# A ConvNeXt V2 block on one core: PSUM tiles of 2, 1 and 1 banks for the expansion, and a new order of the tensor engine's work inside a block

## The chip, the core and the metric

The kernel runs on one core of a Trainium2 chip. A core has five engines that each work through a queue of their own in program order: TensorE (PE, matrix products, with its weight loads shown apart as PEld), VectorE (DVE), ScalarE (ACT), GpSimd (POOL) and SyncE (SP), which here only issues DMAs. Matrix products land in PSUM, a small memory of 8 banks, each of which holds 512 float32 numbers in every partition; ACT and DVE read it. The metric is the device time of one execution in microseconds (us), as the median of several runs; lower is better.

## The reference

The input is one image of 512 by 512 pixels with 96 channels. Cut to what matters:

```python
xp = pad(x)                                        # one pixel all round
out = sum(xp[:, i:i+H, j:j+W, :] * dw[i, j] for i in range(3) for j in range(3))
h = layernorm(out, axis=-1)                        # over the 96 channels, eps 1e-5
h = gelu(einsum('bhwc,ce->bhwe', h, w1))           # 96 -> 384 channels
gx = sqrt((h * h).sum(axis=(1, 2)) + 1e-6)         # one number per channel, over ALL pixels
nx = gx / (gx.mean(axis=-1) + 1e-6)
h = grn_gamma * (h * nx) + grn_beta + h
return x + einsum('bhwe,ec->bhwc', h, w2)          # 384 -> 96 channels
```

The sum of squares over all pixels splits the work into two passes: nothing of the second product can start before every pixel has been through the gelu.

## The kernel before

The image is cut into 128 blocks of four rows (`GR = 4`, `NBLK = 128`), 2048 pixels each.

**Pass one** walks over slots `s` (the loop at line 721). A slot does the convolution of one block and, some slots later in the life of a block, each further stage of it: the slot in which a stage runs is put down beforehand in a table (`put`, lines 687 to 714), and `get(kind)` asks for the blocks that are due. So one slot holds the convolution of block `s`, the statistics of an earlier block, the normalising of a still earlier one, and the expansion (`mlp`) of one earlier again. Every engine's instructions are kept in program order (`InOrder`), so the order of the lines in the slot body (lines 779 to 816) is the order on the engine.

- Convolution: `conv_taps` gives three bursts of 24 small matmuls (64 by 32 tiles of the array) into three PSUM banks of the pool `psY`, and `evac`, one ACT copy of those banks to `y_bf`. After bursts 0 and 1 it issues `pe.drain()`.
- LayerNorm: POOL squares `y_bf` (`stage_sq`), PE sums over channels (`stage_stats`, 24 small matmuls), a short chain on POOL and DVE makes 1/sigma, SP carries it through memory to all partitions, and POOL multiplies (`stage_norm`). The normalised block is written to memory and read back transposed (`stage_write`, `stage_read`).
- Expansion: 96 to 384 channels in three groups of 128 (`NCH = 3`), over four quarters of 512 pixels. Two quarters, or three, are made channel-major (`cm_quads`: three in two blocks of three, two in the others), the rest pixel-major. `pair(j)` makes the first two quarters of channel group `j`: two matmuls into a two-bank tile `U` of the pool `psU`, which has two such tiles, and one gelu of 1024 columns into `gsh`. `rest(n)`, three times, makes the rest in the same manner into `gm`. A block thus fills 12 banks in six two-bank tiles, each with one ACT instruction.
- Squares: DVE takes the statistics of channel-major quarters (`squares`, `squares_rest`); the pixel-major ones are squared by PE (`gram_mms`: 12 matmuls for a block with three channel-major quarters, 24 for one with two), one slot later.

PSUM in pass one is full: one bank for sums and Gram (`SG`), four for `psU`, three for `psY`.

The body of a slot with an expansion, before, is

```python
conv(0); pair(0); pair(1)
squares(0)
conv(1); spread_out(); turn_x(s + 2)
pair(2); squares(1)
conv(2); evac()
rest(0); squares(2); stats
rest(1); gram of the block before
rest(2); squares_rest()
```

**Pass two** (line 898) takes the blocks again. Only the first quarter's gelu was stored; the other three are made anew (`recompute_units`, three units `fresh(j)` of a block, each three matmuls and one gelu of 1536 columns), then `stage_mm2` multiplies with the scaled `w2` in four sub-steps of 12 by 4 matmuls, and DVE adds the residual `xb` that POOL prepared. `pace` (line 330), called after each sub-step, says how many units are to have been issued by then: `LEAD` is 8 units at the start, `even` rises with the sub-steps, and `advance` issues what is missing. The last two blocks (`is_res`) are kept on chip and come first in pass two; their units are made at the end of pass one, with a tile of `psU`.

Of the kernel before, what the change touches and what calls it, by code (L numbers as in the profile page):

```python
# [9 lines left out]
ACTF = mybir.ActivationFunctionType  # L10
# [43 lines left out]
def kernel(  # L54
# [33 lines left out]
    def is_res(q):  # L88
        return q >= NBLK - RES
# [13 lines left out]
    def quad(flat_ap, t):  # L103
        return flat_ap.rearrange("p r (t g m) -> p t g r m", t=NQ, m=MB)[:, t]

    def quad_out(flat_ap):
        return flat_ap.rearrange("p (g r m) -> p g r m", r=GR, m=MB)
# [52 lines left out]
    with ExitStack() as p1:  # L160
# [2 lines left out]
        gmpool = p1.enter_context(tc.tile_pool(name="gm", bufs=3))  # L163
        bstpool = p1.enter_context(tc.tile_pool(name="bst", bufs=2))
        psS = p1.enter_context(tc.tile_pool(name="psS", bufs=1, space=bass.MemoryType.PSUM))
        psU = p1.enter_context(tc.tile_pool(name="psU", bufs=2, space=bass.MemoryType.PSUM))
        pc = p1.enter_context(ExitStack())
        psY = pc.enter_context(tc.tile_pool(name="psY", side="right", bufs=1, space=bass.MemoryType.PSUM))
        xinpool = pc.enter_context(tc.tile_pool(name="xin", side="right", bufs=4))
# [84 lines left out]
        def recompute_units(q):  # L254
            nk = kept_quads(q)
            ynt = grp[q]["ynt"]

            def fresh(j):
                if j == 0:
                    grp[q]["made"] = late.gr.tile([128, NCH, (NQ - 1) * QW], bf16, name="gr")  # L260
                if is_res(q):
                    U = psU.tile([128, 2, QW], f32, name="U")
                else:
                    U = late.psU2.tile([128, NQ - 1, QW], f32, name="U2")
                for t in range(nk, NQ):
                    pe.matmul(quad_out(U[:, t - nk, :]), lhsT=w1p[:, j * 128:(j + 1) * 128],
                               rhs=quad(ynt[:], t), start=True, stop=True)
                n = (NQ - nk) * QW
                act.activation(out=grp[q]["made"][:, j, :n], in_=U[:].rearrange("p k w -> p (k w)")[:, :n],
                                func=ACTF.Gelu_apprx_tanh)  # L270

            return [lambda j=j: fresh(j) for j in range(NCH)]

# [55 lines left out]

        def pace(n, sub):  # L330
            due = sum(1 for v in todo if v <= n + 1) if sub == NSUB - 1 else 0
            even = LEAD + (n * NSUB + sub + 1) * (total + 2 - LEAD) / (NSUB * NBLK)
            advance(max(due, even), n + PRE)

        SG = psS.tile([128, 2 * NS + NCH * 128], f32, name="SG")
# [6 lines left out]
                pe.matmul(J[:, k % NI, :], lhsT=zrow[:, :128], rhs=zrow[:], start=True, stop=True)  # L342

        busy(FILL[0])
        Ud = psU.tile([128, 2, W], f32, name="U")[:, 0, :NI * 9].rearrange("p (i k) -> p i k", i=NI)
        for i in range(NI):
            dve.tensor_copy(out=dwx[:, i], in_=dw9[:, None, chans(i)].to_broadcast([9, GR, 32]))
            pe.matmul(Ud[:, i, :], lhsT=dwx[:, i].rearrange("p q c -> p (q c)"), rhs=ident_b[:9, :9],
# [58 lines left out]

        def conv_taps(b, spare):
            if spare:
                Ua = psU.tile([128, 2, W], f32, name="U")  # L410
                Ub = psU.tile([128, 2, W], f32, name="U")
                Y = [Ua[:, 0, :], Ua[:, 1, :], Ub[:, 0, :]]
            else:
                Y3 = psY.tile([128, NI, W], f32, name="Y")
                Y = [Y3[:, i, :] for i in range(NI)]
            mms = []
            for n in range(3):
                mms.append([(h, j, (n + h) % NI, dx) for dx in (0, -1, 1) for j in range(GR) for h in range(2)])
            flat = [m for ms in mms for m in ms]
            first = {}  # L420
            last = {}
            for n, (h, j, i, dx) in enumerate(flat):
                first.setdefault((i, j), n)
                last[i, j] = n

            def burst(n):
                k = sum(len(ms) for ms in mms[:n])
                for h, j, i, dx in mms[n]:
                    src = b + shift(h, j)
                    o0, o1 = max(0, -dx), W - max(0, dx)  # L430
                    pe.matmul(
                        Y[i][32 * j:32 * j + 32, o0:o1],
                        lhsT=Wq[64 * h:64 * h + 64, i, dx + 1, j, :],
                        rhs=x_rows(src, 64 * h, 64 * h + 64, i, MB * (1 + dx) + o0, o1 - o0)
                        if 0 <= src < NBLK else zrow[64 * h:64 * h + 64, o0:o1],
                        start=first[i, j] == k,
                        stop=last[i, j] == k,
                    )
                    k += 1
                if n < 2:  # L440
                    pe.drain()

            def evac():
                y = ypool.tile([128, NI, W], bf16, name="y_bf")
                if spare:
                    act.activation(out=y[:, 0:2, :], in_=Ua[:], func=ACTF.Identity)
                    act.activation(out=y[:, 2, :], in_=Ub[:, 0, :], func=ACTF.Identity)
                else:
                    act.activation(out=y[:], in_=Y3[:], func=ACTF.Identity)
                ybf[b] = y  # L450

            return [lambda n=n: burst(n) for n in range(3)], evac

        def stage_sq(b, on_act):
            q = ysqpool.tile([128, NI, W], bf16, name="ysq")
# [80 lines left out]
        def stage_spread(k):  # L536
            n = BATCHES[k][1]
            wide = rns.pop(k)
            U = psU.tile([128, 2, W], f32, name="U")
            for bb in range(n):  # L540
                for g in range(NG):
                    pe.matmul(U[:, bb, g * 128:(g + 1) * 128],
                              lhsT=wide[:, bb, g].rearrange("p j c -> p (j c)"), rhs=ident_b[:],
                              start=True, stop=True)
            rbc = rbcpool.tile([128, BATCH, W], bf16, name="rbc")
            act.activation(out=rbc[:, :n, :], in_=U[:, :n, :], func=ACTF.Identity)
            rbcs[k] = rbc
# [60 lines left out]
        def px0(b):  # L608
            return NCH * QW * (cm_quads(b) - 2)

        def mlp_units(b):
# [4 lines left out]
            def cm_mm(dst, j, t):  # L616
                pe.matmul(quad_out(dst), lhsT=w1p[:, j * 128:(j + 1) * 128], rhs=quad(yt[:], t), start=True, stop=True)

            def pair(j):
                U = psU.tile([128, 2, QW], f32, name="U")  # L620
                for t in range(2):
                    cm_mm(U[:, t, :], j, t)
                act.activation(out=gsh[:, :, j, :], in_=U[:], func=ACTF.Gelu_apprx_tanh)

            def rest(n):
                U = psU.tile([128, 2, QW], f32, name="U")
                Uf = U[:].rearrange("p k w -> p (k w)")
                c0 = 2 * QW * n
                c, end = c0, c0 + 2 * QW
                while c < end:  # L630
                    if c < px0(b):
                        j, sz = c // QW, QW
                        cm_mm(Uf[:, c - c0:c - c0 + sz], j, 2)
                    else:
                        k, e0 = divmod(c - px0(b), E)
                        sz = min(E - e0, 512 - c % 512, end - c)
                        t, r = divmod(k, GR)
                        col = (cm_quads(b) + t) * 128
                        pe.matmul(Uf[:, c - c0:c - c0 + sz], lhsT=yt[:, r, col:col + 128], rhs=w1p[:, e0:e0 + sz],
                                  start=True, stop=True)  # L640
                    c += sz
                act.activation(out=gms[b][:, c0:end], in_=Uf, func=ACTF.Gelu_apprx_tanh)
# [16 lines left out]
            def store():  # L659
                sp.dma_start(out=g_dram[b], in_=gsh[:, 0].rearrange("p j w -> p (j w)"))  # L660

            return pair, rest, squares, squares_rest, store

        def gram_mms(b):
            for k in range((TAIL - px0(b)) // E):
                for j in range(NCH):
                    c = px0(b) + k * E + j * 128
                    v = gms[b][:, c:c + 128]
                    pe.matmul(gram[:, j, :], lhsT=v, rhs=v, start=False, stop=True, skip_group_check=True)
# [51 lines left out]
        for s in range(last_slot + 1):  # L721
# [55 lines left out]
                    gram_mms(b)  # L777
            else:
                b = mlp[0]
                pair, rest, squares, squares_rest, put_out = mlp_units(b)  # L780
                conv = lambda n: taps[n]() if taps else None
                conv(0)
                pair(0)
                pair(1)
                if not taps:
                    for b2 in get("gram"):
                        if b2 != b:
                            gram_mms(b2)
                squares(0)
                conv(1)  # L790
                spread_out()
                if s + 2 < NBLK:
                    turn_x(s + 2)
                pair(2)
                squares(1)
                for k in get("turn"):
                    stage_turn(k)
                conv(2)
                if evac:
                    evac()  # L800
                rest(0)
                squares(2)
                for b2 in get("stats"):
                    stage_stats(b2)
                rest(1)
                if taps:
                    for b2 in get("gram"):
                        if b2 != b:
                            gram_mms(b2)
                rest(2)  # L810
                squares_rest()
                for b2 in get("gram"):
                    if b2 == b:
# [126 lines left out]
```

## Time and profile before

| what | before |
|---|---|
| median of 10 runs | 1566.81 us (1562.33 to 1570.31) |
| the profiled execution | 1565.02 us |
| its span, from the first instruction to the last | 1563.2 us |
| busy share of the span: PE, ACT, POOL, DVE | 93%, 93%, 84%, 72% |
| pass one with convolution and expansion in each slot | from about 206 to 935 us |
| slots with expansion alone | about 935 to 1018 us |
| pass two | about 1022 us to the end |

The page gives busy time by engine. A busy share is an average over passes with different limits, and the ends of matmuls are modelled, so 93% on PE does not mean that PE is at its peak. What a slot costs is better read from the times at which the same instruction comes round again: in the stretch from 205.99 to 935.06 us the ACT instruction that empties the convolution (`y_bf`) comes 98 times. Two mean times per instruction matter in what follows: the gelu of two banks into `gsh` has a mean of 1025 ns over 378 instructions, that of three banks in pass two 1457 ns over 378.

In a timeline line, the first number is the start in us from the start of the span, the second the length in us of what was merged into the line, then come engine, source line, operation, output, inputs, shape and count; in square brackets stands the idle time before it and what ended that.

### The profile page before, as it was taken

To read this page: it belongs to the slowest core of one execution; us is meant where nothing else is said; L and a number is where in the kernel's file an instruction comes from. 1 tells how busy PE (TensorE), PEld (TensorE's weight loads), DVE (VectorE), ACT (ScalarE), POOL (GpSimd) and SP (SyncE) were. 2 spreads that over 40 slices of the span, in tenths; PEclk is the share of its full clock that TensorE was granted. 3 is DMA by queue.
4 is the path that set the end of the run, shared out by engine and by line. 5 is a ranking of instruction groups with operands and counts; after the bars stand their busy time and mean duration, and the time that the engine had idled before them with its cause. 6 is when DMAs were issued, how large, how long until landed. Compare 5 with 4: busy or idle time off the path is not lost. (4 is left out here: it accounts for less than half of the span.)

```text
span 1563.2 us, 55720 instructions
## 1 busy us (share of the span) xinstructions
PE 1450.0 (93%) x23749; PEld 844.2 (54%) x23749; DVE 1129.7 (72%) x2027; ACT 1447.2 (93%) x1306; POOL 1314.2 (84%) x933
## 2 busy tenths in 40 slices
PE   7889999999999999999999997789999999999997
PEld 2434444444444444444444444457777777777765
DVE  6748978889898888889888888855555555555544
ACT  3879989999999999999999999999999999999997
POOL 3559888998989898998889887559999999999994
PEclk8999999999999999999999999999999999999999
DMA  5668787787778788777878767879999999999993
GB/s 149 181 179 266 224 255 229 231 251 231 220 238 257 214 246 246 222 240 231 256 209 243 221 189 225 263 259 387 386 389 390 393 385 392 387 380 382 385 372 147
DMA packets 235470, 427.94 MB, mean 274 GB/s; under 512 B 34102, under 2 KB 148374, under 8 KB 235222
## 3 DMA queue, kind: packets, MB, share of 16 engines
q1 hardware_dynamic: 219972, 356.59, 70.4%
q0 software_dynamic: 13888, 67.64, 11.4%
q8 instruction: 186, 3.05, 0.8%
q14 instruction: 62, 0.51, 0.1%
q10 hardware_dynamic: 1362, 0.15, 0.1%
HBM read 272.78 MB, written 150.72 MB: 271 GB/s over the span
## 5 line engine op out<-in xcount | busy, mean ns | idle before, releaser
L32 PE MATMUL U<-ynT,w1p 128*128 128x512 bf16 x2166 | 601.8, 380 | 44.0 <-ACT gm L32 8.4
L32 DVE BATCH_NORM_STATS2 bst<-gsh 128x6 f32<-128x512 bf16 x756 | 468.8, 673 | 129.4 <-ACT gsh L32 128.8
L32 ACT ACTIVATE gr<-U 128x1536 bf16<-128x1536 f32 (+1 forms) x384 | 521.0, 1451 | 15.9 <-PE U L32 13.9
L32 POOL TENSOR_TENSOR yn<-y_bf,rbc 128x1536 bf16<-128x1536 bf16 x128 | 397.0, 3104 | 87.8 <-DMA rbc<-r_dram 32.7
L32 DVE TENSOR_TENSOR o_sb<-O,xb 128x384 bf16<-128x384 f32 x512 | 277.6, 557 | 252.1 <-PE O L32 180.0
L278 POOL TENSOR_TENSOR xb<-xr,B2c 128x1536 f32<-128x1536 bf16 x126 | 394.9, 3134 | 37.8 <-DVE B2c L32 29.7
L32 ACT ACTIVATE gsh<-U 128x1024 bf16<-128x1024 f32 x378 | 369.5, 1025 | 55.4 <-ACT gm L32 29.8
L32 ACT ACTIVATE gm<-U 128x1024 bf16<-128x1024 f32 x384 | 367.9, 1036 | 0.1
L32 PE MATMUL Y<-xT,Wq 64*32 64x511 bf16 (+1 forms) x8694 | 321.5, 389 | 10.2 <-DVE B2bc_f L32 3.7
L32 POOL TENSOR_TENSOR ysq<-y_bf 128x1536 bf16<-128x1536 bf16 x114 | 313.3, 2748 | 13.6 <-ACT y_bf L32 13.5
L32 PEld LDWEIGHTS <-w1p 128*128 128x128 bf16 x2166 | 169.2, 97 | 277.7 <-issue 174.0
L32 PEld LDWEIGHTS <-gr 128*128 128x128 bf16 x4584 | 228.7, 98 | 84.4 <-ACT gr L32 12.1
L32 PE MATMUL O<-W2s,gr 128*128 128x96 bf16 x4584 | 251.4, 206 | 12.1 <-ACT gr L32 9.4
L32 PEld LDWEIGHTS <-Wq 64*32 64x32 bf16 x9216 | 102.3, 90 | 189.1 <-issue 148.6
L32 PE MATMUL U<-w1p,ynT 128*128 128x384 bf16 (+2 forms) x1032 | 161.3, 272 | 34.1 <-ACT gm L32 31.2
L32 ACT ACTIVATE y_bf<-Y 128x1536 bf16<-128x1536 f32 x121 | 175.2, 1448 | 17.9 <-PE Y L32 17.7
L32 DVE STREAM_TRANSPOSE xT<-xin 128x576 f32<-128x576 f32 (+1 forms) x256 | 181.4, 748 | 4.0 <-DMA xin<-in_x_dram 2.9
L32 DVE BATCH_NORM_STATS2 bst<-gm 128x6 f32<-128x512 bf16 x252 | 156.5, 677 | 0.9 <-ACT gm L32 0.9
L32 PEld LDWEIGHTS <-ynT 128*128 128x128 bf16 x1032 | 88.6, 96 | 91.4 <-issue 70.0
L32 PE MATMUL SG<-gm 128*128 128x128 bf16 x2064 | 136.3, 219 | 0.5 <-ACT gm L32 0.3
L32 PEld LDWEIGHTS <-gm 128*128 128x128 bf16 x2064 | 121.0, 98 | 11.5 <-issue 0.5
L250 POOL DMA_DIRECT2D xr<-in_x_dram x123 | 67.6, 549 | 27.6 <-POOL xb L278 27.6
(103 smaller groups left out, 700.3 us busy)
## 6 DMA issues: line engine op xcount, KB each, us to landing
ynT<-yn_dram SPq DMA_DIRECT2D x254, 384.0 KB
xin<-in_x_dram SPq DMA_DIRECT2D x126, 432.0 KB
yn_dram<-yn SPq DMA_DIRECT2D x512, 96.0 KB
xr<-in_x_dram POOLq DMA_DIRECT2D x128, 384.0 KB, 6.6
out_dram<-o_sb SPq DMA_DIRECT2D x127, 384.0 KB
g_dram<-gsh SPq DMA_DIRECT2D x126, 384.0 KB
gl<-g_dram SPq DMA_DIRECT2D x84, 384.0 KB
gl<-g_dram POOLq DMA_DIRECT2D x42, 384.0 KB, 6.6
```

Of the source, the lines that this page charges most:

```text
L32: r = f(*a, **k)
L250: pq.dma_start(out=xr[:], in_=x[0, r0:r0 + GR].rearrange("r w c -> (r w) c").rearrange("(p g) c -> p g c", g=PXP))
L278: pq.tensor_tensor(out=xb[:], in0=grp[q]["xr"][:], in1=bias[:, None, :].to_broadcast([128, PXP, C]), op=ALU.add)
```

## The change

Pass one's pool `psU` (two tiles of two banks) becomes two pools: `psU2` with one tile of two banks and `psU1` with two tiles of one bank. `banks(n)` takes a tile of the wanted size. The six two-bank units of a block become nine: in banks, 2, 1, 1, 2, 1, 1, 2, 1, 1, each with its own matmuls and its own gelu (`unit(bank, n)` in place of `pair` and `rest`). The matmuls themselves are the same ones.

The order in the slot changes: `conv(1)` is issued without its drain; the Gram matmuls of the block before are cut into two halves (`gram_mms(b, part)`), one after the third channel group's unit, one after the third convolution burst; the third burst and `evac` move behind the first two units of `gm`; the statistics matmuls go between the last two units but one and the last. `squares(2)` stands between the two one-bank units of `gm`.

In pass two, `even` now rises by `total` over all sub-steps in place of `total + 2 - LEAD`, so the lead of 8 units is held until the units run out. The units of the two kept blocks, made in pass one's PSUM, are cut in the same manner (`half`). The setup tile, the spare convolution tiles and `stage_spread` take theirs from `banks`.

The number of channel-major quarters (`cm_quads`) is the same on both sides of this diff.

```diff
-        psU = p1.enter_context(tc.tile_pool(name="psU", bufs=2, space=bass.MemoryType.PSUM))
+        psU2 = p1.enter_context(tc.tile_pool(name="psUa", bufs=1, space=bass.MemoryType.PSUM))
+        psU1 = p1.enter_context(tc.tile_pool(name="psUb", bufs=2, space=bass.MemoryType.PSUM))
+
+        def banks(n):
+            return (psU2 if n == 2 else psU1).tile([128, n, W], f32, name=f"U{n}")
...
+                if not is_res(q):
+                    half(late.psU2.tile([128, NQ - 1, QW], f32, name="U2"), nk, NQ)
+                elif j % 2:
+                    half(banks(1), nk, nk + 1)
+                    half(banks(1), nk + 1, NQ)
                 else:
-                    U = late.psU2.tile([128, NQ - 1, QW], f32, name="U2")
...
+                    half(banks(2), nk, NQ)
...
-            even = LEAD + (n * NSUB + sub + 1) * (total + 2 - LEAD) / (NSUB * NBLK)
+            even = LEAD + (n * NSUB + sub + 1) * total / (NSUB * NBLK)
...
-                Ua = psU.tile([128, 2, W], f32, name="U")
-                Ub = psU.tile([128, 2, W], f32, name="U")
+                Ua, Ub = banks(2), banks(1)
...
-                if n < 2:
+                if n < 2 and fence:
                     pe.drain()
...
-            def pair(j):
-                U = psU.tile([128, 2, QW], f32, name="U")
-                for t in range(2):
-                    cm_mm(U[:, t, :], j, t)
-                act.activation(out=gsh[:, :, j, :], in_=U[:], func=ACTF.Gelu_apprx_tanh)
-
-            def rest(n):
-                U = psU.tile([128, 2, QW], f32, name="U")
+            def unit(bank, n):
+                U = banks(n)
+                if bank < 2 * NCH:
+                    j, t0 = divmod(bank, 2)
+                    for t in range(t0, t0 + n):
+                        cm_mm(U[:, t - t0, :], j, t)
+                    act.activation(out=gsh[:, t0:t0 + n, j, :], in_=U[:], func=ACTF.Gelu_apprx_tanh)
+                    return
                 Uf = U[:].rearrange("p k w -> p (k w)")
-                c0 = 2 * QW * n
-                c, end = c0, c0 + 2 * QW
+                c = c0 = (bank - 2 * NCH) * QW
+                end = c0 + n * QW
...
-        def gram_mms(b):
-            for k in range((TAIL - px0(b)) // E):
+        def gram_mms(b, part=None):
+            n = (TAIL - px0(b)) // E
+            for k in range(n) if part is None else range(n // 2) if part == 0 else range(n // 2, n):
...
+                def gram_of_last(part):
                     for b2 in get("gram"):
                         if b2 != b:
-                            gram_mms(b2)
+                            gram_mms(b2, part)
+
+                conv(0)
+                unit(0, 2)
+                unit(2, 1)
                 squares(0)
-                conv(1)
+                conv(1, False)
                 spread_out()
                 if s + 2 < NBLK:
                     turn_x(s + 2)
-                pair(2)
+                unit(3, 1)
+                unit(4, 2)
                 squares(1)
+                gram_of_last(0)
+                unit(6, 1)
+                squares(2)
+                unit(7, 1)
                 for k in get("turn"):
                     stage_turn(k)
                 conv(2)
                 if evac:
                     evac()
-                rest(0)
-                squares(2)
+                gram_of_last(1)
+                unit(8, 2)
+                unit(10, 1)
                 for b2 in get("stats"):
                     stage_stats(b2)
-                rest(1)
-                if taps:
-                    for b2 in get("gram"):
-                        if b2 != b:
-                            gram_mms(b2)
-                rest(2)
+                unit(11, 1)
                 squares_rest()
```

## The prediction

> **What bounds the kernel now.** I read the busy time by stretch first, since the two passes have different limits; the columns are the stretch, its length, then busy time and (count) of PE, PEld, DVE, ACT and POOL, the granted clock, the DMA share and GB/s.
>
> ```profile
> 205.99:935.06 729.07, 684.61 (x12400) 343.16 (x12399) 628.62 (x1066) 683.21 (x680) 643.93 (x485) 1.00 0.77 234
> 935.06:1018.00 82.94, 61.93 (x541) 36.20 (x540) 70.66 (x119) 79.29 (x86) 52.51 (x36) 1.00 0.78 239
> 1032.00:1488.00 456.00, 453.40 (x6409) 331.28 (x6408) 243.51 (x451) 452.19 (x333) 427.45 (x260) 1.00 1.03 382
> 1488.00:1563.20 75.20, 62.55 (x854) 44.31 (x850) 33.72 (x62) 60.41 (x44) 52.96 (x28) 1.00 0.69 254
> ```
>
> In the first stretch PE and ACT are both busy 94% and neither is at its end: they wait for each other. From 1032 to 1488 ACT works without a gap (452 of 456 us), and after 1488 it does not. The first stretch holds 97 slots, so a slot takes 729.07 / 97 = 7.516 us. Who waits is seen in the timeline, of ACT (first fence) and of PE (second).
>
> ```profile
> 604.02 1.45 ACT L32 ACTIVATE y_bf<-Y 128x1536 bf16<-128x1536 f32 x1
> 605.37 2.85 ACT L32 ACTIVATE gm<-U 128x1024 bf16<-128x1024 f32 x3
> 608.64 2.93 ACT L32 ACTIVATE gsh<-U 128x1024 bf16<-128x1024 f32 x3 [0.42 <-ACT gm L32]
> 611.46 1.45 ACT L32 ACTIVATE y_bf<-Y 128x1536 bf16<-128x1536 f32 x1
> 612.79 2.93 ACT L32 ACTIVATE gm<-U 128x1024 bf16<-128x1024 f32 x3
> 616.27 2.92 ACT L32 ACTIVATE gsh<-U 128x1024 bf16<-128x1024 f32 x3 [0.55 <-PE U L32]
> ```
>
> ```profile
> 602.45 0.60 PE L32 MATMUL U<-ynT,w1p 128*128 128x512 bf16 x2
> 602.98 0.89 PE L32 MATMUL Y<-xT,Wq 64*32 64x512 bf16 x24
> 603.80 0.61 PE L32 MATMUL U<-w1p,ynT 128*128 128x384 bf16 x4
> 605.28 0.83 PE L32 MATMUL SG<-gm 128*128 128x128 bf16 x12
> 606.44 0.60 PE L32 MATMUL U<-w1p,ynT 128*128 128x256 bf16 x4 [0.32 <-ACT gm L32]
> 606.97 0.87 PE L32 MATMUL Y<-xT,Wq 64*32 64x512 bf16 x24
> 607.95 1.03 PE L32 MATMUL U<-ynT,w1p 128*128 128x512 bf16 x4
> ```
>
> The circle is this. ACT empties the convolution at 604.02, before the fourth pair of banks, so the gelu of that pair starts only at 605.37. Both tiles of `psU` are then full, and PE, through with its Gram matmuls at 605.95, waits until 606.44 for the last pair. Then it must do the next convolution burst first (606.97) and reaches the next pair at 607.95; ACT, finished with the last `gm`, has idled until 608.64. With two tiles PE can't run far enough ahead to bridge one 1 us burst.
>
> [...] The trace shows burst 2, which has no drain, at 602.98 with the next matmul at 603.80, 0.82 us; burst 0, with one, at 606.97 and 607.95, 0.98 us. [...]
>
> **The change part by part, pass one.** First the two sums. PE, by starts in the timeline: a bank of expansion 0.216 us (the two-bank line at 602.45 lasts 0.60, a single matmul 0.38), times 12 = 2.59; three bursts of 0.92 each with the 0.10 us of the switch into them (602.45 + 2 x 0.216 = 602.88, burst at 602.98) = 2.76, and two drains 0.32; the statistics 0.60 (604.25 to 604.85); Gram 0.055 a matmul, 0.66 for 12 and 1.32 for 24. That is 6.93 us in a slot with 12 Gram matmuls and 7.59 with 24. Measured are 7.45 and 7.63: two slots of three wait half a us, the third is PE's own work. The change takes out one drain: 6.77 and 7.43, mean 6.99. It adds no matmul; each bank was a matmul group of its own before.
>
> ACT before: three `gsh` at 0.947, three `gm` at 0.903, `y_bf` 1.34 (604.02 to 605.37), together 6.89 us. The change cuts three of six gelus in two. Price of a 512-column gelu from start to start: the page has none. The nearest row is an Identity of 512 columns at the very start, which lasts 0.60 with the next ACT instruction beginning 0.50 later:
>
> ```profile
> 26.98 0.60 ACT L32 ACTIVATE rbc<-U 128x512 bf16<-128x512 f32 x1 [6.01 <-PE U L32]
> 27.48 1.45 ACT L32 ACTIVATE y_bf<-Y 128x1536 bf16<-128x1536 f32 x1
> ```
>
> From below, gelus of 1536 columns come 1.387 apart in pass two (36 in 50.01 us) and of 1024 0.914, which leaves 0.44 for 512; from above, 0.60 if nothing overlapped. [...] I take 0.50 (0.52 into `gsh`, 0.48 into `gm`). ACT's new sum: 2 x 0.947 + 2 x 0.52 + 0.903 + 4 x 0.48 + 1.34 = 7.10, that is 0.21 more.
>
> Now the order. I walk one slot with 12 Gram matmuls, in us from its first burst, with these same prices, 0.165 from the last matmul's slot to its end and 0.09 from there to ACT. PE starts: burst 0 at 0.00, banks 0-1 at 0.98, bank 2 at 1.41, burst 1 at 1.73, bank 3 at 2.55, banks 4-5 at 2.78, half Gram 3.22, bank 6 at 3.55, bank 7 at 3.82, burst 2 at 4.14, half Gram 4.96, banks 8-9 at 5.29, bank 10 at 5.72, statistics 5.94, bank 11 at 6.53, next burst 0 at 7.10. ACT starts: 1.72, 2.67, 3.19, 3.71, 4.66, 5.14, `y_bf` 5.62, 6.96, 7.86, 8.34, and the next slot's first gelu is wanted at 8.82: its banks were filled at 8.08 + 0.43 + 0.17 = 8.68. ACT never waits, because `y_bf` now follows two one-bank units, whose banks it sets free early, and PE fills three units while ACT is behind. So this slot ends at ACT's floor, 7.10. One with 24 Gram matmuls ends at PE's, 7.39 with what ACT has in hand from the slot before. The mean is (7.10 + 7.39 + 7.10) / 3 = 7.20. The same walk for the old order gives 7.49, 7.59, 7.49, close to the measured 7.45, 7.63, 7.44, which is why I trust it. Gain: 0.316 us x 108 such slots (97, and 11 more between 110 and 193 us) = 34.1 us. With 0.44 for the short gelu the walk gives 7.01 and 55 us; with 0.50 and the missing drain worth nothing, 7.26 and 28 us.
>
> What else is on the way. POOL: four slots of work, 27.57 us from the normalising at 451.18 to that at 478.75, without a wait, 6.89 a slot; under 7.20, so it is cover with 0.3 us left. DVE: 628.62 / 97 = 6.48. Its `squares(2)` now stands before the transposition of 1/sigma, but after instructions that are done by then. The later `y_bf` (by about 1.5 us in the slot) reaches POOL's squaring one slot on, where POOL already waits for it in places (0.32 us at 500.35), and the statistics come two slots on; each has a whole slot of room. SP gets the same DMAs in the same order, sooner by 4%; a DMA share of 0.77 leaves room. The single two-bank tile is asked for again only after two one-bank units and a burst, so it is free by then (the walk has it so). Slots without convolution: 5.55, or 6.2 where a 0.62 us wait for Gram stands in them, 5.86 in the mean of 13; after, ACT's 7.10 less `y_bf`, about 5.8: nothing. The ramp (first 110 us) and the two kept blocks have one large tile fewer and a few short gelus more: I put 1 us.
>
> **Pass two.** The chain at the end, ACT:
>
> ```profile
> 1488.87 4.24 ACT L32 ACTIVATE gr<-U 128x1536 bf16<-128x1536 f32 x3 [0.22 <-PE U L32]
> ...
> 1533.19 2.79 ACT L32 ACTIVATE gr<-U 128x1536 bf16<-128x1536 f32 x2 [0.51 <-PE U L32]
> 1537.38 4.13 ACT L32 ACTIVATE gr<-U 128x1536 bf16<-128x1536 f32 x3 [1.40 <-PE U L32]
> ```
>
> While the lead falls from 8 units to 2, ACT begins to wait: five times 0.22, six times 0.51, four times 1.40, 9.8 us in all from 1488 on. Held at 8 units, as it is at the start of the pass where ACT has no gap, these go: the last gelu ends near 1548 in place of 1558. The last unit is then issued when 8 + 0.75 k reaches 384, at sub-step 502 of 512, so ten sub-steps of 12 matmuls remain where before two did (8 + 0.738 k); at 0.65 us each from about 1545.6 they end at 1552 instead of 1560.1. Gain 8 us. If POOL's `xb` or the loads held it, less; at least 0. POOL waited there for freed buffers (2.23 us at 1539.68), so it has room.
>
> **Sum.** -34.1 - 8 + 1 = -41.1 on a span of 1563.2; from the median, which stands 1.8 us over the profiled 1565.02, 1566.8 - 41 = 1526.
>
> **Rivals.**
> Half held back: POOL waits 43 us between 400 and 900 us (25.7 for the sums, 15.6 for 1/sigma or a free buffer, 1.8 for `y_bf`), 0.65 us a slot. If part of it is latency and not lead, POOL becomes the bound: 6.89 + half of 0.65 = 7.2, and with stalls handed on some 7.36. Against: two batches from 451 to 493 us have none. 108 x 0.156 = 17, with pass two and the ramp 1542.
> Tail alone: all of that wait stays (6.89 + 0.65 = 7.54), pass one keeps its time, pass two gives 8: 1558.
> Slower: a gelu of 512 columns takes its whole 0.60 from start to start. ACT's floor is 6.89 + 3 x (1.20 - 0.925) = 7.70, nothing can hide it, and 108 x 0.184 = 20, less 8, plus 1, is +13: 1580. It decides from 0.58, where a slot costs 7.59 and pass two's gain is eaten. For it: ACT is within 8% of its floor already. Against: the 0.50 above.
> That three channel-major quarters come in every block is not in the diff (`cm_quads` stays), so I count nothing for it.
>
> **How the numbers follow.** Forecast 53%, half held back 19%, tail alone 12%, slower 16%. The likeliest gives 1526, with its own range 1505 (short gelu 0.44) to 1536 (the drain worth nothing, half of pass two's gain). No change that can be told is within 0.2%, 3 us: a third of the tail case, 4%. Faster 80%, slower 16%. For 8 in 10 the range takes in the first two rivals and leaves out the slower one: 1505 to 1560.
>
> **What would show it.** Right: `y_bf` comes every 7.1 to 7.3 us, gelus of 512 columns start 0.5 apart, ACT idle at the slot's start is gone, ACT shows no gaps after 1488. Wrong: 512-column gelus 0.6 apart; POOL without a gap; PE waiting for `gm` as before; the two-bank tile late.

## The result, and the profile after

| | before | after |
|---|---|---|
| median | 1566.69 us (32 runs) | 1549.35 us (9 runs, 1547.12 to 1553.64) |
| ratio of the runs | | 0.9891, 95% interval 0.988 to 0.9903 |
| profiled execution, its span | 1565.02, 1563.2 us | 1552.5, 1550.7 us |

The change makes the kernel faster by 1.1%, 17 us where 41 were forecast. Busy times by stretch, in the columns of the prediction's first fence, with the stretches cut at the same events as before (the first holds the same 97 slots):

```profile
206.42:925.08 718.66, 682.19 (x12410) 349.57 (x12408) 628.85 (x1066) 688.35 (x972) 648.66 (x491) 0.99 0.78 238
925.08:1008.70 83.62, 63.93 (x555) 37.23 (x553) 72.48 (x123) 83.57 (x131) 48.74 (x35) 1.00 0.80 253
1020.00:1476.00 456.00, 446.05 (x6259) 324.53 (x6258) 238.67 (x439) 446.55 (x330) 418.21 (x253) 1.00 1.02 374
1476.00:1550.70 74.70, 68.71 (x1005) 50.77 (x1001) 39.37 (x73) 63.83 (x47) 63.99 (x35) 1.00 0.83 307
```

The 97 slots took 729.07 us and now take 718.66. The gain is 10.4 us, where 30.6 were forecast for these 97. In the long stretch of pass two ACT had been busy 452 of 456 us; now it is busy for 446.55. From the first gelu of pass two to the end the profiled executions need 540.8 us before (1022.38 to 1563.2) and 541.0 after (1009.70 to 1550.7): pass two gained nothing, where 8 us were forecast.

The gelus themselves do what the walk had them do. ACT's timeline after:

```profile
609.74 2.92 ACT L32 ACTIVATE gsh<-U 128x1024 bf16<-128x1024 f32 x4 [0.30 <-ACT gm L32]
612.51 1.12 ACT L32 ACTIVATE gm<-U 128x512 bf16<-128x512 f32 x2
613.47 1.51 ACT L32 ACTIVATE y_bf<-Y 128x1536 bf16<-128x1536 f32 x1
614.80 2.08 ACT L32 ACTIVATE gm<-U 128x1024 bf16<-128x1024 f32 x3
```

Four `gsh` units start at 609.74 and the next group at 612.51, 2.77 us later. Two of the four are short. A whole one takes 0.90 to 0.92 us from start to start in this trace, so a short one costs (2.77 - 0.92 - 0.90) / 2 = 0.475. The two short `gm` units take 0.96 from start to start, 0.48 each. The price taken, 0.50, was a little high, and the rival that wanted 0.60 is out. The idle time at the slot's head, about 0.4 to 0.55 us in every slot before, is now some 0.3 us in one slot of three and absent in nearly all others. By the starts of `y_bf`, the slots take 7.45, 6.97 and 7.08 us in turn, over and over, with a mean of 7.204 over 89 of the 97. The other eight, every twelfth, take 9.1 to 10.5 us each and together 77.5, which is 19.9 us more than eight usual ones. That is what is missing in the first stretch. Here is one of them, cut from all engines in order of time:

```profile
617.47 2.77 DVE L32 BATCH_NORM_AGGREGATE mv<-bst 128x2 f32<-128x192 f32 x3
617.57 0.87 PE L32 MATMUL U<-ynT,w1p 128*128 128x512 bf16 x3
...
620.15 0.23 DVE L32 TENSOR_SCALAR mom<-SG 128x128 f32<-128x128 f32 x1
...
620.48 0.17 DVE L32 MEMSET SG<- 128x128 f32 x1
...
620.69 0.49 PE L32 MATMUL SG<-gm 128*128 128x128 bf16 x6 [2.26 <-DVE SG L32]
...
621.50 1.09 ACT L32 ACTIVATE gm<-U 128x512 bf16<-128x512 f32 x2 [1.82 <-PE U L32]
```

PE is through with its expansion units at 618.4 and the first Gram half is next. That half adds into the columns of `SG` behind the LayerNorm sums, and it waits until DVE has copied and cleared those sums, at 620.65. DVE does this once in four slots (`stage_moments`), at the head of a slot. Every twelfth slot, the three aggregations of the squares (`combine`) stand just ahead of it and make it 2.77 us later. Then PE stands still for 2.26 us, and ACT waits behind it for 1.82.

The wait is not all that such a slot loses. In four of the eight, the granted clock of PE then stands at half for 3.4 us; this begins between 0.2 us before and 1.1 us after the end of the wait. Those four slots take 9.6 to 10.5 us, the other four 9.1 to 9.4. Two stretches of equal length behind such a wait, the first with and the second without (columns as above; the kinds of matmul in them are not the same):

```profile
797.20:800.60 3.40, 3.40 (x39) 1.72 (x39) 3.40 (x6) 1.27 (x3) 2.66 (x10) 0.50 0.92 295
620.70:624.10 3.40, 3.40 (x72) 2.40 (x71) 3.40 (x6) 2.60 (x4) 2.66 (x10) 1.00 0.74 245
```

By the means of the two kinds, 10.19 and 9.19 us, about 16 of the 19.9 us are the wait and about 4 the clock; this is an estimate.

In pass two, POOL's timeline shows what else is new. `gl` is the stored first quarter of a block and `xr` the input from which `xb` is made. Before:

```profile
1187.63 3.14 POOL L278 TENSOR_TENSOR xb<-xr,B2c 128x1536 f32<-128x1536 bf16 x1
1190.70 0.56 POOL L245 DMA_DIRECT2D gl<-g_dram  x1
1191.26 0.54 POOL L250 DMA_DIRECT2D xr<-in_x_dram  x1
1191.81 3.13 POOL L278 TENSOR_TENSOR xb<-xr,B2c 128x1536 f32<-128x1536 bf16 x1
```

After:

```profile
1187.26 3.14 POOL L287 TENSOR_TENSOR xb<-xr,B2c 128x1536 f32<-128x1536 bf16 x1
1190.70 0.56 POOL L255 DMA_DIRECT2D xr<-in_x_dram  x1 [0.30 <-POOL xb L287]
1191.25 0.54 POOL L250 DMA_DIRECT2D gl<-g_dram  x1
1191.81 3.13 POOL L287 TENSOR_TENSOR xb<-xr,B2c 128x1536 f32<-128x1536 bf16 x1
```

The load of `xr` can be issued only when the `xb` just ahead of it has read the buffer, and it starts 0.30 us after the end of that instruction. With the `gl` issue between them this wait is covered and the step takes 4.18 us; with `xr` first it takes 4.55. Nobody wrote this order down: in pass two the loads and `xb` are handed to the bare engine (`nc.gpsimd`), not to the `InOrder` wrapper of pass one, and the build places them. In the traces 28 of 41 `gl` issues stand ahead of their `xr` before, none after. Three blocks now cost POOL 12.54 us, 4.18 each. Apart from the waits of 0.30 us and one of 2.53 us (at 1331.97, for PE, ahead of a `gl` issue), it works without a break to the end:

```profile
1524.66 3.13 POOL L287 TENSOR_TENSOR xb<-xr,B2c 128x1536 f32<-128x1536 bf16 x1
1528.09 0.55 POOL L255 DMA_DIRECT2D xr<-in_x_dram  x1 [0.30 <-POOL xb L287]
1528.67 15.44 POOL L287 TENSOR_TENSOR xb<-xr,B2c 128x1536 f32<-128x1536 bf16 x5
```

The last `xb` ends at 1544.11, and the last matmuls follow until 1546.60. From the first `xb` with the final bias to the fifth from the end POOL needs 509.4 us (1019.29 to 1528.67). Before it needed 496.6 (1031.07 to 1527.67) and then waited for freed buffers. ACT's gaps at the end are gone as forecast, but a gap of 0.22 us stands in every third block:

```profile
1514.92 12.32 ACT L32 ACTIVATE gr<-U 128x1536 bf16<-128x1536 f32 x9 [0.22 <-PE U L32]
1527.46 13.54 ACT L32 ACTIVATE gr<-U 128x1536 bf16<-128x1536 f32 x10 [0.22 <-PE U L32]
```

Nine gelus every 12.54 us are POOL's rhythm.

### The profile page after: what moved, and what is told of

Same layout as the page of the kernel before. It is cut to its first block, busy times and chain, and to the rows that moved or that the text cites. A ratio compares the mean times of both kernels' runs of the same rounds, so it can differ in the third digit from the quotient of the medians.

```text
span 1550.7 us, 56008 instructions
## 1 busy us (share of the span) xinstructions
PE 1448.5 (93%) x23749; PEld 851.3 (55%) x23749; DVE 1129.9 (73%) x2027; ACT 1453.2 (94%) x1692; POOL 1315.4 (85%) x933
## 5 line engine op out<-in xcount | busy, mean ns | idle before, releaser
L32 PE MATMUL U<-ynT,w1p 128*128 128x512 bf16 x2166 | 607.9, 380 | 35.9 <-ACT gm L32 7.8
L32 ACT ACTIVATE gm<-U 128x512 bf16<-128x512 f32 (+1 forms) x640 | 413.0, 770 | 15.8 <-PE U L32 15.6
L32 PE MATMUL Y<-xT,Wq 64*32 64x511 bf16 (+1 forms) x8694 | 326.4, 393 | 22.3 <-ACT y_bf L32 4.9
L32 PEld LDWEIGHTS <-gr 128*128 128x128 bf16 x4584 | 237.0, 98 | 106.3 <-issue 19.8
L32 PE MATMUL O<-W2s,gr 128*128 128x96 bf16 x4584 | 257.5, 206 | 11.8 <-DVE o_sb L32 11.3
L32 PEld LDWEIGHTS <-Wq 64*32 64x32 bf16 x9216 | 109.4, 91 | 195.0 <-issue 149.3
L32 ACT ACTIVATE y_bf<-Y 128x1536 bf16<-128x1536 f32 x121 | 184.1, 1521 | 22.3 <-PE Y L32 20.4
L32 PEld LDWEIGHTS <-gm 128*128 128x128 bf16 x2064 | 128.1, 98 | 102.7 <-issue 71.5
L32 PE MATMUL SG<-gm 128*128 128x128 bf16 x2064 | 159.4, 221 | 18.3 <-DVE SG L32 17.9
L32 PEld LDWEIGHTS <-ynT 128*128 128x128 bf16 x1032 | 81.4, 98 | 30.8 <-issue 6.5
```

The costliest lines, as they stand in the source:

```text
L32: r = f(*a, **k)
```

## The experiments

Two theories were to be tested, each against its rivals. Theory A says that the long slots come from the first Gram half waiting for the clearing. Theory C says that POOL is the bound of pass two in the changed kernel, through the order of its DMA issues (C2).

**The aggregations one slot later**, in the changed kernel. All work is the same; DVE's aggregations no longer precede the clearing.

```diff
-                put(m, "combine", b)
+                put(m + (b < NBLK - 1), "combine", b)
```

> The changed kernel with DVE's three aggregations (bn_aggr, 2.77 us together, every twelfth slot) put one slot later, so that they no longer stand on DVE just ahead of the copy and clearing of the LayerNorm sums, for whose clearing the first Gram half waits. Theory A (Gram waits for the clearing, which shares its PSUM bank): the eight or nine slots of 9.1 to 10.4 us go, all slots have a mean of 7.2, and the time falls by about 22 us to 1527. Theory B (the long slots come from POOL's or the DMAs' latency on the way to 1/sigma): they stay, 1549.

Measured: 1529.76 us, ratio to before 0.9751 (0.9729 to 0.9772), 19.6 us under the changed kernel. DVE's timeline, with the clearing first and the aggregations behind:

```profile
603.21 0.27 DVE L32 TENSOR_SCALAR mom<-SG 128x128 f32<-128x128 f32 x1
603.59 0.17 DVE L32 MEMSET SG<- 128x128 f32 x1
...
608.49 2.77 DVE L32 BATCH_NORM_AGGREGATE mv<-bst 128x2 f32<-128x192 f32 x3
```

No slot of the 97 is longer than 7.5 us, and their mean is 7.169. From 200 to 800 us the granted clock is 1.00 in each stretch of 200 us, where it was 0.98, 0.99 and 0.99 in the changed kernel with its stretches of half clock. Theory A holds; the forecast's walk had 7.20.

**The same edit in the kernel before**, as the control.

> The kernel before with the aggregations one slot later and nothing else: the control for theory A. There Gram stands behind the statistics and late in the slot, when DVE has long cleared the sums, so nothing waits for an aggregation: no difference, 1565 to 1568. If the aggregations cost time by DVE's load alone (theory B2), it gains as the changed kernel did, 20 us.

Measured: 1566.23 us, ratio 1.0 (0.9991 to 1.0009). In the kernel before, PE waits for the clearing in eight of the 97 slots, at most 0.3 us and ahead of the statistics. In this run these waits are gone, and the time is the same. It is the new place of the Gram matmuls that makes the aggregations cost 20 us.

**All `gl` loads by SP**, in the changed kernel.

```diff
-                (pq if q % 3 == 0 else sq).dma_start(
+                sq.dma_start(
```

> The changed kernel with all loads of gl in pass two issued by SP, none by POOL. Theory C (POOL is the bound of pass two: three blocks cost it 12.54 us, of which 0.52 are the gl issue): POOL needs 4.01 us a block, PE's own 4.03 becomes the bound, pass two is some 11 us shorter, 1538. Theory D (PE and ACT set pass two, POOL's busy time is cover): 1549. If SP's queue becomes late with the 42 loads more, slower than 1549.

Measured: 1533.46 us, ratio 0.9779 (0.9759 to 0.9799), 15.9 us under the changed kernel, more than the 11 expected. One event may be part of the excess: in the changed kernel POOL waits 2.53 us for PE at 1331.97, and just after it PE stands for 2.89 us (until 1336.3) and then has half the clock for 3.4 us. In this run POOL has no such wait.

**POOL's order as written**, in the changed kernel: pass two's loads and `xb` go through the wrapper that keeps program order. These are the same instructions in another order.

```diff
-            stage_load(n + PRE, nc.sync, nc.gpsimd)
+            stage_load(n + PRE, nc.sync, pool)
...
-            stage_xb(ORDER[n + 2], nc.gpsimd, B2c)
+            stage_xb(ORDER[n + 2], pool, B2c)
```

> The changed kernel with POOL's instructions of pass two kept in the order of the program: all 41 gl issues stand before xr. Nothing is added or taken away. Theory C2 (the order costs 0.36 us each time): three blocks cost POOL 12.19 in place of 12.54 us, PE's 4.03 a block is then the bound or nearly, 10 to 12 us faster, 1538. Theory D (order is of no account): 1549.

Measured: 1534.42 us, ratio 0.9783 (0.9767 to 0.9799), 14.9 us under the changed kernel. So it is the order that costs the time, since nothing was taken off POOL. But the run changes more of the order than the places of `gl`, as POOL's timeline shows:

```profile
1184.81 3.12 POOL L32 TENSOR_TENSOR xb<-xr,B2c 128x1536 f32<-128x1536 bf16 x1 [0.41 <-DVE o_sb L32]
1187.87 0.56 POOL L32 DMA_DIRECT2D gl<-g_dram  x1
1188.42 0.54 POOL L32 DMA_DIRECT2D xr<-in_x_dram  x1
1188.98 3.13 POOL L32 TENSOR_TENSOR xb<-xr,B2c 128x1536 f32<-128x1536 bf16 x1
1192.04 0.56 POOL L32 DMA_DIRECT2D xr<-in_x_dram  x1
1192.87 3.12 POOL L32 TENSOR_TENSOR xb<-xr,B2c 128x1536 f32<-128x1536 bf16 x1 [0.27 <-DVE o_sb L32]
```

The wait of 0.30 us is gone ahead of every `xr`, also where no `gl` stands. In the order as written, one more `xb` lies between an `xr` and the `xb` that reads its buffer; in the order of the build that `xb` stands just ahead (122 of 123 times in the changed kernel, and before too). POOL now waits for DVE to free its buffers, so it is no longer the bound. The expectation's 12.19 us for three blocks was therefore too high; its time, 1538, was off by 4. What the 28 changed places of `gl` cost by themselves this run does not show; 28 x 0.37 us = 10 is an estimate from the two steps above.

**The new pace alone**, in the kernel before.

```diff
-            even = LEAD + (n * NSUB + sub + 1) * (total + 2 - LEAD) / (NSUB * NBLK)
+            even = LEAD + (n * NSUB + sub + 1) * total / (NSUB * NBLK)
```

> The kernel before with the new pace of pass two alone. The prediction's step (ACT's 9.8 us of gaps at the end go, nothing else moves): 8 us faster, 1558.7. Theory C2: the build orders POOL's instructions in pass two anew with the pace, 28 of 41 gl issues then stand between the xr issue and xb instead of before xr, which costs POOL 0.36 us each, 10 us: the two cancel, 1565 to 1568, with POOL busy to the end.

Measured: 1565.24 us against 1566.69, ratio 0.9993 (0.9985 to 1.0001). Its trace has all 41 `gl` issues behind `xr`, as in the changed kernel, so this one line is what turns the order round. ACT's gaps of 0.51 and 1.40 us at the end are gone, and POOL works to the end: what the pace gains is given back on POOL.

**The old pace in the changed kernel** undoes that part alone.

> The changed kernel with the old pace of pass two. The prediction's step: ACT's gaps at the end come back and it is 8 us slower, 1557. Theory C2: with the old pace the old order of POOL's instructions comes back too, worth 10 us the other way, so 1547 to 1551.

Measured: 1549.89 us, 0.5 us from the changed kernel's 1549.35, ratio to before 0.9891 (0.9866 to 0.9917). Its trace has 28 `gl` issues ahead of `xr` again, and ACT's gaps at the end. So the new pace is worth nothing that these runs can tell in the change as it stands.

**The drain back**, in the changed kernel: `conv(1)` in place of `conv(1, False)`.

> The changed kernel with the drain after burst 1 put back. If PE has no slack at all in a slot, 0.16 us x 108 = 17 us slower, 1566; by the walk (slot mean 7.26 against 7.20, ACT being the bound in two slots of three) 6.5 us slower, 1556; if a drain comes with the change of tiling mode anyway, no difference, 1549.

Measured: 1560.06 us, ratio 0.9951 (0.9934 to 0.9968), 10.7 us over the changed kernel, between the walk's 6.5 and the 17 of a PE without slack. The slots under 8 us have a mean of 7.287 us against 7.194 in the changed kernel, where the walk had 7.26 against 7.20. So 0.093 x 108 = 10 us are in those; 0.093 is somewhat over half of the 0.16 us that the drain takes on PE (0.98 us from burst to next matmul with it, 0.82 without, in the trace before). The expectation's last case, no difference, is out.

**The old tiles in the new order**, with the drain: two tiles of two banks, six units.

```diff
-            return (psU2 if n == 2 else psU1).tile([128, n, W], f32, name=f"U{n}")
+            return psU.tile([128, 2, W], f32, name="U")[:, :n, :]
...
-                unit(2, 1)
+                unit(2, 2)
...
-                unit(3, 1)
                 unit(4, 2)
                 squares(1)
                 gram_of_last(0)
-                unit(6, 1)
+                unit(6, 2)
                 squares(2)
-                unit(7, 1)
...
-                unit(10, 1)
...
-                unit(11, 1)
+                unit(10, 2)
```

> The changed kernel with the old PSUM tiles, two of two banks, six units of two banks in the new order (banks 0, 2, 4, 6, 8, 10), and with the drain after burst 1. To be held against the run that has the drain back and the new tiles. By the walk a slot then takes 7.43 against 7.26 us, 18 us slower than that run, about 1574: the tiles earn more than the three cut gelus cost. If the new order alone does it, no slower than that run, or faster by the 0.2 us a slot that ACT saves.

Measured: 1576.05 us, ratio to before 1.0051 (1.003 to 1.0071), so 16 us over the run with the drain and the new tiles, and slower than before. The slots under 8 us have a mean of 7.435 us; the walk had 7.43. This kernel has eight long slots as well, 9.2 to 10.5 us. The new order alone loses: its usual slots are 0.08 us shorter than the 7.516 before, and the long ones, with about 20 us, outweigh that. The tiles carry the largest part of what a usual slot gains: about 0.08 us come from the order, 0.15 from the tiles and 0.09 from the drain left out.

**Both repairs together**: aggregations later, `gl` by SP.

> The changed kernel with the aggregations one slot later and all gl loads issued by SP. If the two losses are independent, as theories A and C have it: 22 + 11 us, 1516. If POOL or the DMAs hold pass one once the long slots are gone: 1525 to 1535.

Measured: 1509.80 us, ratio to before 0.9641 (0.9614 to 0.9667): 39.5 us under the changed kernel, 57 under the one before. The two single gains make 19.6 + 15.9 = 35.5, and together they give at least that, as two independent losses would. Its chain of waits holds no POOL:

```profile
PE 34%; DVE 0%; issue 0%
```

**The old pace there**, where POOL is out of the way.

> The fastest kernel so far (aggregations later, gl by SP) with the old pace. POOL is no longer in the way there, so the prediction's step about pass two can show: ACT's gaps at the end come back, 8 us slower, 1518. If the pace is worth nothing even then: 1510.

Measured: 1525.48 us, 15.7 us over the run with both repairs. In the profiled executions pass two takes 538.0 us against 525.1, so 12.9 us of it are seen there; this execution also has one slot of 10.34 us in pass one, which has nothing to do with the pace. ACT's gaps are back in the same sizes as in the kernel before, here the first of each size:

```profile
1450.68 4.24 ACT L32 ACTIVATE gr<-U 128x1536 bf16<-128x1536 f32 x3 [0.22 <-PE U L32]
...
1471.81 4.13 ACT L32 ACTIVATE gr<-U 128x1536 bf16<-128x1536 f32 x3 [0.51 <-PE U L32]
...
1499.20 4.13 ACT L32 ACTIVATE gr<-U 128x1536 bf16<-128x1536 f32 x3 [1.40 <-PE U L32]
```

Five, six and four of them make 9.8 us, as in the prediction. The rest can come from the distance between gelus ahead of the gaps. With the new pace and both repairs no gap stands in

```profile
1249.24 245.95 ACT L32 ACTIVATE gr<-U 128x1536 bf16<-128x1536 f32 x183
```

that is (245.95 - 1.45) / 182 = 1.343 us from start to start. With the old pace it is 1.358 even in the stretch without gaps (332 gelus in 450.95 us from 999.52). So the old pace costs a little long before it shows as a gap.

**`gl` by SP in the kernel before.**

> The kernel before with all gl loads issued by SP. POOL gets 12.03 us for three blocks, but the old pace still ends with ACT's 9.8 us of gaps. Theory: the middle of pass two gains what POOL held up there, 3 to 5 us, 1562. If POOL alone set the end: 8 us and more, under 1559. If the end hangs on the pace alone: 1566.

Measured: 1562.74 us, ratio 0.9978 (0.9969 to 0.9987), 3.5 us faster. ACT's gaps at the end are still there: the pace, not POOL, holds the end. Freeing POOL is worth 16 us with the new pace and 3.5 without; the pace is worth 13 to 16 with POOL freed and nothing without.

**The drain of burst 0 moved** to just ahead of burst 1, in the kernel with both repairs.

> The fastest kernel so far with the drain of burst 0 moved from behind that burst to just ahead of burst 1, behind three banks of expansion. If an explicit drain there costs what it cost behind the burst (0.16 us), no difference, 1510; if most of it falls together with the drain of the switch into burst 1, PE gains up to 0.1 us in the one slot of three that it bounds and ACT's banks come 0.16 us sooner: 3 to 6 us faster, 1505.

Measured: 1513.48 us, ratio 0.9658 (0.9629 to 0.9688), an interval that overlaps that of the run without the move. The slots have a mean of 7.174 against 7.170 us: as far as four runs each can tell, the explicit drain costs the same in either place. That the switch into burst 1 drains PE too was the author's assumption; no run shows it.

## Why the prediction was right in sign and wrong in size

**Bound of pass one, right.** PE and ACT waiting for each other at the slot's head, and the tiles as the cure: the run with the old tiles in the new order is 16 us slower for want of them, and slots of 7.435, 7.287 and 7.194 us stand against the walk's 7.43, 7.26 and 7.20. That the mean fits so well is in part luck: the two slots of three that ACT bounds take 6.97 and 7.08 us where the walk had 7.10, and the one that PE bounds takes 7.45 for 7.39.

**Price of a short gelu, right enough:** 0.48 for the 0.50 taken. The 0.50, with its 0.52 into `gsh` and 0.48 into `gm`, was the author's estimate between 0.44 and 0.60, and no run shows the difference between the two: after the change both start 0.48 us apart. The slower rival needed 0.58. The 0.44 that the prediction worked out from below was too low: it took gelus of 1536 columns at 1.387 us apart, and they come at 1.343 where nothing holds them back.

**The missing drain, right:** about 0.09 us a slot against the walk's 0.06. The 0.10 us that the sum puts down to the switch into a burst are the distance, in one place of the timeline before, from the two expansion matmuls' 2 x 0.216 us (602.88) to the start of the burst (602.98); no run shows its cause.

**What else is on the way, wrong, and the larger failure.** The prediction went through DVE with one sentence, a busy sum of 6.48 us a slot and one moved instruction. It counted the Gram halves as PE time only. Gram and the LayerNorm sums are parts of one tile, `SG`, in one bank, and DVE clears the sums at the head of every fourth slot. In the kernel before, Gram stood behind the statistics, late in the slot. The change moves it ahead of them and leaves it a quarter of a microsecond behind the clearing's usual time (cleared at 603.76, Gram at 604.01 in the run with later aggregations), and the aggregations take 2.77. The step should have named what stands ahead of the clearing on DVE. The trace before had a sign of it. Among its waits from 206 to 935 us (us in total, times, longest) stands PE waiting for DVE on `SG`:

```profile
PE SG L32 <- DVE SG L32: 2.3, 8, 0.3
```

These are the same clearings, in every twelfth slot, met there by the statistics. With up to 2.77 us for each of eight, the size of the loss, 19.9 us in 97 slots, could have been estimated. That half the clock would follow some of the waits could not be read from the trace before, which has no such stretch among these slots. In the trace of the changed kernel the Gram half waits 2.26 us for the clearing though the two touch different columns of the tile.

**Pass two, wrong.** The mechanism is real: ACT's gaps go, and with POOL out of the way the pace earns 13 to 16 us, more than the 8 put down. What failed is the sentence that POOL has room because it waited for freed buffers at the end. Those waits, 5 us in all, were less than the 12.8 us more that POOL needs in its new order, and it was not asked whether that order is fixed. Of the 12.8, some 10 are the 28 places of `gl` at 0.37 us each; 2.53 are the one wait for PE, which all five traces with this order have and no other. The chain of waits before had a warning in it: POOL's `xb` held 8.8% of the span, more than twice the 3.3% of ACT's `gr`.

**The ramp, too small:** put at 1 us, it cost 3.5 (the fifteenth convolution is emptied at 101.2 us, before at 97.75). Most of that arises in one early slot (`y_bf` at 49.20 for 45.56, from 38.65 and 38.64). It takes 10.55 us for 6.92, and in 7.6 of the 10.55 the granted clock is at half. In this slot the run with the later aggregations, the one with both repairs and the one with the moved drain take 8.3 to 8.4 us, the one with the drain back 10.73. So about 1.5 us belong to the change, and the rest of the slot's 3.6 goes with the lower clock of this execution; this is an estimate. **The slots without convolution** gained about 1.8 us where nothing was put down: 5.72 us in the mean of 13 (928.26 to 1002.61) for 5.86.

The sum of the profiled spans: ramp +3.5, the slots from there to 206 us -3.0, the 97 slots -10.4, from there to pass two -2.7, pass two +0.2: -12.4, and the spans differ by 12.5. The medians differ by 17.3, since the profiled execution of the changed kernel is among the longest of its nine. The mean granted clock was lower after the change, 0.989 over its runs for 0.994 to 0.995 before. Within the kernel before, runs at 0.990 to 0.997 take 1571.8 to 1562.2 us, so 0.005 of clock goes with about 6 us; this is an estimate, and it overlaps with the clock's part of the long slots and of the ramp.

**The rivals.** The result lies nearest to "half held back", 1542, but its reason was not the one given: POOL's latencies in pass one were never in the way. With Gram's wait removed, POOL's own waits were still there and the slots took 7.169 us.

## What to carry to other kernels

When an instruction moves forward in its queue, look at every tile that it reads or writes and ask which other engine last touches any part of that tile (here other columns of `SG`, a wait of 2.26 us), and what stands ahead of that on the other engine in the worst slot, not the mean one; the cost shows in one slot of twelve and no sum of busy times shows it. Where instructions go to an engine without a fixed order, an edit to one queue can rearrange another (here the 28 of 41 `gl` issues ahead of `xr` became none): compare the orders in the two traces before crediting a gain, and fix the order where a wait depends on it. A gain behind two limits at once (here POOL and the pace) shows little when either alone is lifted (3.5 us and nothing here, and some 16 us in pass two with both lifted): before dropping such an edit as worthless, try it with the other limit out of the way.

## What was not expected of the hardware

In these traces a DMA issue on POOL directly behind an instruction that it depends on costs 0.30 us of idle time besides its own 0.55, and another issue of 0.54 between the two hides that wait. Gelus of 512 columns out of one bank start 0.48 us apart and those of 1024 columns 0.90 to 0.92, so each cut cost ACT about 0.05 us.

The granted clock fell to half after some stands of PE. Between the first 100 us and the last 3 us, the trace of the changed kernel has five such stretches of 3.4 us each. Each begins between 0.2 us before and 1.1 us after the end of a stand of PE: four at one of Gram's waits for the clearing, each of 2.26 us, and one behind the stand of 2.89 us that ends at 1336.3. Not every stand is followed by one: the other four of the eight waits, of 2.04 to 2.26 us, are not. The trace of the kernel before has no such stretch between these times, though PE stands there for 1.13 us five times from 1534.91 on. What decides between the cases stays open.
